# Weight splitting, copy placement and instruction order in an attention and two-MoE kernel

## The chip, the cores and the metric

The kernel runs on one core of one Trainium2 chip. The metric is the device time of one execution in microseconds, as a median over executions. Engines are called by their names and, in profile rows, by short ones: TensorE (PE, its weight loads PEld), VectorE (DVE), ScalarE (ACT), GpSimd (POOL), SyncE (SP, its queue SPq). L455 is line 455 of the kernel before.

## The reference

Three stages in float32 follow each other. Attention has 4 batches, 8 heads, 576 positions and 64 features. Its output is a coarse part (queries, keys and values averaged over groups of 4 positions, softmax attention on 144 of them, each result repeated 4 times) plus a local part (softmax over the at most 7 positions with a distance under 4). The result, 2304 tokens by 512, goes through two dense layers:

```python
h = x @ w_in                       # first MoE: 512 -> 2048
r = np.maximum(h, 0.0)
x = (s * (r * r) + b) @ w_out      # 2048 -> 512
out = ((x @ w_a) * (x @ w_b)) @ w_out2   # second MoE: 512 -> 1536 -> 512
```

The inputs of the change are the weights w_in and w_out of the first MoE. The host hands all weights over as 64-bit words (float64 bit patterns in the kernel's eyes: two 32-bit words, or four 16-bit halves).

## The kernel before, in words

TensorE multiplies in fp32r, a float32 format that it reads in rounded form. To keep float32 accuracy every operand is split into a high part (the value copied into fp32r) and a low part (the value minus its high part), and a product takes three matmuls: high by high, high by low, low by high.

The first MoE goes over six blocks of 384 tokens (BLOCKS). In each block 16 steps (a_iter) run over the 2048 hidden columns, 128 at a time: 12 matmuls make h (L1162 to L1164), ScalarE takes relu (L1179), square (L1183) and the high copy gh (L1186), VectorE the low part gl (L1190), and 12 matmuls add to four output banks (L1205 to L1207). One step needs two weight slices, one of w_in and one of w_out, so 32 slices in all; they stay in SBUF after the first block. The second MoE begins at about 504 us of the span.

A slice is prepared by w_words and w_slice, in this order: SyncE loads 512 KB (L335, w); ScalarE scales the upper words to z (L414); ScalarE moves the low bits out of the second half of each pair of words (L421); VectorE tests the sign and writes it as a half word (L426); VectorE shifts z by 3 and ors low bits and sign in (L434); ScalarE copies z to the high part (L450); VectorE subtracts for the low part (L455). RAMP_BUFS gives z two buffers.

Ahead of the first block and beside it runs attention. Batch 0 and the first 768 tokens ("ramp") are done with matmuls: down() handles the coarse part of one batch and head pair (scores L688, row maximum L702, exponential L715, transposes L739, copies L751, output L760, copy to upT L772), tile_job() the local part of 128 tokens (scores L843 and L851, maximum L878, subtraction L887, exponential L895, sum L919, division L925 and L929, transposes L937, copies L947, output L956, sum with the coarse part x L973). split_x() then makes the high part xsh on ScalarE (L569) and the low part xsl on VectorE (L573). The first three tiles feed block 0. The values of batch 1 are averaged over 4 positions by transfers: pool_in() has SyncE load two halves plainly (L621) and GpSimd add six more on top with adding transfers (L623), each one behind the one before on the same half; down(1, ...) needs them in L760. GpSimd also averages K and Q of batch 1 (L656, L657). Later tokens get their local part from VectorE alone (unit()).

The order of instructions on each engine is not written by hand. Every piece of work is a Task with an engine, an estimated duration, what it reads and writes, buffers and PSUM banks that it takes and gives back, and a due time. Program.order() simulates the engines and picks, again and again, the task that can start first; between equals the earlier due time decides. Class Wire estimates transfers and class Clock TensorE's clock. What this simulation decides is then the fixed order on every engine and every buffer's owner; engines wait on semaphores for what isn't there yet, in order. T0, LEAD and the DUE_ constants shift due times. While no h matmul has run, the simulation puts filler matmuls (L330, bf16 zeros, up to 20 at a time) in front of TensorE tasks that would otherwise leave it idle; they write a bank of the group "acc" that is held until the first h.

These lines of order() hold the rule:

```python
key = (s + t.wait, t.due - t.lead, t.num, s)
if best is None or key < best[0]:
    best = (key, t, picks, fs)
```

## Time and profile before

| what | value |
|---|---|
| runs | 928.06, 933.91, 927.93 us; median 928.06 |
| profiled execution | 933.64 us |
| its span | 931.8 us, so 1.84 us lie around the span |
| granted TensorE clock, mean over the span | 0.988 |
| TensorE busy | 909.6 us, 98% |
| VectorE busy | 781.5 us, 84% |
| ScalarE busy | 480.9 us, 52% |
| GpSimd busy | 72.4 us, 8% |
| DMA | 97.07 MB, mean 104 GB/s |

The span is the time from the first to the last instruction of the profiled execution; all stretches below count from its start. A PEclk of 1.00 is TensorE's upper level of 2.4 GHz, 0.50 its lower level of 1.2 GHz; a value between them is a mean over a stretch. Durations of neighbouring instructions on one engine overlap by a little, so what one instruction costs its engine is read from the distance between starts. A row with x2 merges two instructions of one kind.

### The profile page before, as it was taken

What the parts mean: (1) busy time and instruction counts of PE and PEld (TensorE: products, weight loads), DVE (VectorE), ACT (ScalarE), POOL (GpSimd) and SP (SyncE); (2) the same over time, 40 slices, a digit from 0 to 9 for tenths busy, and PEclk for the clock granted to TensorE, in tenths of its full rate; (3) what the DMA queues carried; (4) which work ended last, traced back from release to release, by engine and by line L of the source; (5) the groups of instructions that cost most, each with busy time, mean ns of one, the idle gap of its engine ahead of it and who ended that gap; (6) DMA issues with size and microseconds to landing.
All of it is one profiled execution on the core that took longest, in us unless ns stands there. A gap on an engine that the chain in (4) does not pass through costs nothing.

```text
span 931.8 us, 14461 instructions
## 1 busy us (share of the span) xinstructions
PE 909.6 (98%) x5456; PEld 847.6 (91%) x5456; DVE 781.5 (84%) x1383; ACT 480.9 (52%) x1017; POOL 72.4 (8%) x73
## 2 busy tenths in 40 slices
PE   8996999999999999999999999999999999999998
PEld 5685999999999899999999899998999999999997
DVE  7995898999999999995977999779877779877753
ACT  4694994335544454445987545336433336433322
POOL 0531122002222210000000000000000000000000
PEclk9997999999999999999999999999999999999999
DMA  9972936224345432314667232002200000200001
GB/s 244 273 258 62 289 89 206 82 69 128 105 118 116 133 89 69 102 29 161 213 228 256 93 107 75 23 23 102 86 23 26 26 11 35 102 23 24 1 1 68
DMA packets 47145, 97.07 MB, mean 104 GB/s; under 512 B 6396, under 2 KB 21884, under 8 KB 46692
## 3 DMA queue, kind: packets, MB, share of 16 engines
q1 hardware_dynamic: 39444, 93.09, 30.9%
q0 software_dynamic: 7200, 2.67, 2.4%
q8 instruction: 43, 0.70, 0.3%
q10 hardware_dynamic: 432, 0.39, 0.1%
q14 instruction: 26, 0.21, 0.1%
HBM read 83.54 MB, written 12.58 MB: 103 GB/s over the span
## 4 chain that ended last, share of the span: by engine, by line
PE 81%; DVE 8%; issue 5%; DMA 3%; POOL 2%; ACT 1%; SPq 0%; DVEq 0%; POOLq 0%; ACTq 0%
PE ab L1451 29%; PE acc L1205 6%; PE acc L1206 6%; PE acc L1207 6%; PE h L1162 6%; PE h L1163 5%; PE acc L1592 5%; PE h L1164 5%; PE acc L1593 5%; PE acc L1591 5%; DVE pr L1072 1%; PE o L760 1%; DMA x<-x2d 1%; DVE gl L1190 1%; DMA w<-in_qT_dram 1%
## 5 line engine op out<-in xcount | busy, mean ns | idle before, releaser
L1451 PE MATMUL ab<-xo,w 128*128 128x384 f32 x1332 | 270.2, 339 | 0.0
L1451 PEld LDWEIGHTS ab<-xo,w 128*128 128x128 f32 x1332 | 239.0, 188 | 16.0 <-DVE u L1525 1.7
L1205 PE MATMUL acc<-gh,w 128*128 128x384 f32 (+1 forms) x384 | 132.6, 345 | 1.0 <-ACT w L421 0.6
L1162 PE MATMUL h<-xsh,w 128*128 128x384 f32 x384 | 132.4, 345 | 0.0
L1206 PE MATMUL acc<-gl,w 128*128 128x384 f32 x384 | 130.1, 339 | 0.4 <-DVE gl L1190 0.4
L1207 PE MATMUL acc<-gh,w 128*128 128x384 f32 (+1 forms) x384 | 129.9, 338 | 0.0
L1163 PE MATMUL h<-xsl,w 128*128 128x384 f32 x384 | 129.8, 338 | 0.0
L1164 PE MATMUL h<-xsh,w 128*128 128x384 f32 x384 | 129.7, 338 | 0.0
L1179 ACT ACTIVATE u<-h 128x384 f32<-128x384 f32 x96 | 47.1, 491 | 124.3 <-PE h L1164 121.5
L1567 ACT ACTIVATE gh<-u 128x384 fp32r<-128x384 f32 x68 | 35.6, 524 | 86.7 <-DVE u L1528 50.2
L1205 PEld LDWEIGHTS acc<-gh,w 128*128 128x128 f32 x384 | 72.3, 188 | 4.5 <-issue 1.9
L1162 PEld LDWEIGHTS h<-xsh,w 128*128 128x128 f32 x384 | 72.6, 189 | 2.0 <-issue 1.8
L1206 PEld LDWEIGHTS acc<-gl,w 128*128 128x128 f32 x384 | 72.5, 189 | 0.9 <-DVE gl L1190 0.8
L1163 PEld LDWEIGHTS h<-xsl,w 128*128 128x128 f32 x384 | 72.8, 189 | 0.0
L1164 PEld LDWEIGHTS h<-xsh,w 128*128 128x128 f32 x384 | 72.6, 189 | 0.0
L1207 PEld LDWEIGHTS acc<-gh,w 128*128 128x128 f32 x384 | 72.5, 189 | 0.0
L1475 ACT ACTIVATE w<-ab 128x384 f32<-128x384 f32 x33 | 16.2, 491 | 100.6 <-PE ab L1451 100.5
L1190 DVE TENSOR_TENSOR gl<-u,gh 128x384 fp32r<-128x384 f32 x96 | 53.0, 552 | 11.5 <-ACT gh L1186 11.1
L1593 PE MATMUL acc<-wx,gl 128*128 128x512 f32 x141 | 55.6, 394 | 0.0
L1592 PE MATMUL acc<-wx,gh 128*128 128x512 f32 x141 | 55.4, 393 | 0.0
L1591 PE MATMUL acc<-wx,gh 128*128 128x512 f32 x141 | 55.4, 393 | 0.0
L426 DVE TENSOR_SCALAR w<-w 128x512 uint16<-128x512 f32 x59 | 42.5, 769 | 11.4 <-ACT w L421 11.4
(205 smaller groups left out, 1712.3 us busy)
## 6 DMA issues: line engine op xcount, KB each, us to landing
w<-in_w_o_dram SPq DMA_DIRECT2D x25, 512.0 KB
w<-in_w_a_dram SPq DMA_DIRECT2D x24, 512.0 KB
bk<-in_ku_dram SPq DMA_DIRECT2D x22, 320.0 KB
bk<-in_vu_dram SPq DMA_DIRECT2D x22, 320.0 KB
w<-wod SPq DMA_DIRECT2D x12, 512.0 KB
w<-in_w_b_dram SPq DMA_DIRECT2D x10, 512.0 KB
x2d<-ev SPq DMA_DIRECT2D x24, 192.0 KB
x<-x2d SPq DMA_DIRECT2D x3, 1536.0 KB
```

The lines of the kernel that those rows point to most:

```text
L1162: nc.tensor.matmul(out=st["h"], lhsT=w[:, 0, k], rhs=hi[:, k], start=(k == 0), stop=False)
L1163: nc.tensor.matmul(out=st["h"], lhsT=w[:, 0, k], rhs=lo[:, k], start=False, stop=False)
L1164: nc.tensor.matmul(out=st["h"], lhsT=w[:, 1, k], rhs=hi[:, k], start=False, stop=(k == HP - 1))
L1179: A_.activation(out=st["u"], in_=st["h"], func=ACTF.Relu)
L1190: V.tensor_tensor(out=st["lo"], in0=st["u"], in1=st["hi"][:, :n].bitcast(F32), op=ALU.subtract)
L1205: nc.tensor.matmul(out=acc, lhsT=wh, rhs=st["hi"], start=(f == 0), stop=False)
L1206: nc.tensor.matmul(out=acc[:, :n], lhsT=wh, rhs=st["lo"], start=False, stop=False)
L1207: nc.tensor.matmul(out=acc, lhsT=wl, rhs=st["hi"], start=False, stop=(f == FA - 1))
L1451: nc.tensor.matmul(out=o, lhsT=w[:, k], rhs=x, start=(not more and k + n == 0), stop=(k == 1 and n == 2), skip_group_check=more,)
L1591: nc.tensor.matmul(out=acc, lhsT=gh, rhs=w[:, 0], start=first, stop=False)
L1592: nc.tensor.matmul(out=acc, lhsT=gh, rhs=w[:, 1], start=False, stop=False)
L1593: nc.tensor.matmul(out=acc, lhsT=gl, rhs=w[:, 0], start=False, stop=last)
```

## The change

For the 32 slices of the first MoE the sign is no longer a test that writes half words. VectorE takes a bitwise and of z with the sign bit, into a new buffer sg of whole contiguous 32-bit words (two of them); ScalarE writes the low bits into the lower halves of these words; the shift and or reads sg. ScalarE's low bits now stand behind the sign, not ahead of it. The second MoE's slices keep the old way. The stage buffer is given back after the low bits, z has three buffers in place of two.

Every third high copy of a slice (H_ENG), all high copies of x in the ramp (XH_ENG) and every third copy to gh in block 0 (Q_ENG) move from ScalarE to VectorE, as copies with one source.

The order is planned anew. The planner's clock counts columns; a class Fetch estimates when TensorE's instructions arrive; adding transfers are taken to land 1.5 us later and to be seen 2 us later; from the ninth to the 96th load on SyncE a load waits in the program itself, too, until the load eight before it has landed (send). Filler matmuls may stand ahead of any TensorE task of the ramp, after the first h too, and write into the task's own bank. All due constants have new values.

```diff
+H_ENG, XH_ENG, Q_ENG = "AAD", "D", "AAD"
-POOL_PREP = 2.0
-CONST_ENG, DUE_CONST = "G", 13.6
+POOL_PREP, VISIT = 2.0, 0.2
+CONST_ENG, DUE_CONST = "G", 9.8
...
-T0, STEP = 32.0, 4.018 / 384
-LEAD = 15.2
-DUE_DOWN = (7.3, 7.1, 8.6, 17.2)
-DUE_NEXT = (57.9, 0.8)
-DUE_TILE = (5.8, 19.7, 21.3)
-DUE_JOB = (12.0, 11.2, 13.0)
-
-WARM, FILL_MIN, FILL_MAX = 18, 0, 20
-
-RAMP_BUFS = {"dq": 2, "dk": 2, "qd": 4, "kd": 4, "tq": 1, "tk": 1, "tv": 1, "e": 1, "x": 1, "z": 2}
+T0, STEP = 29.7, 4.018 / 384
+LEAD = 15.4
+DUE_DOWN = (5.3, 4.2, 19.9, 15.5)
+DUE_NEXT = (62.2, 0.6)
+DUE_TILE = (6.9, 2, 7.1)
+DUE_JOB = (9.7, 11.6, 11.0)
+
+WARM, FILLS, FILL, FILL_COLUMNS, KEEP_COLUMNS = 18, 20, 0.172, 408, 2376.3
+
+RAMP_BUFS = {"dq": 2, "dk": 2, "qd": 4, "kd": 4, "tq": 1, "tk": 1, "tv": 1, "e": 1, "x": 1, "z": 3, "sg": 2}
...
+POOL_LATE = 1.5
+RAMP_QUEUE, RAMP_LOADS, SP_WAIT = 8, 96, 0.15
...
 class Clock:
 
 
-    TICK, COLUMNS = 3.41333, 1.4
+    TICK, FIRST, COLUMNS, KEEP, FULL = 3.41333, 3360.0, 2600.0, KEEP_COLUMNS, 2400.0
+
...
+    def window(self, end):
+        total = 0.0
+        for a, b, cols in reversed(self.past):
+            if b <= end - self.TICK:
+                break
+            total += cols * (b - max(a, end - self.TICK)) / (b - a)
+        return total
...
-            work -= d * rate
-            t += d
+        self.count, self.ready, self.sent = 0, {}, []
+
+    def drain(self, t):
+        return max([b for a, b in self.sent[-24:] if a <= t], default=0.0) - DMA_LAND
+
+    def took(self, drain):
+        return self.FIRST + self.SHARE * max(0.0, drain) + self.TOOK
+
+    def run(self, clock, t, work, cols, words):
+        done = 0
+        for x in range(self.count + 1, self.count + words + 1):
+            i, j = (x + self.EARLY) // self.PART, (x + self.LATE) // self.PART - 1
+            trig, wall = i > 0 and (x + self.EARLY) % self.PART == 0, j > 0 and (x + self.LATE) % self.PART == 0
+            if not trig and not wall:
+                continue
+            n = x - self.count - done
+            t = clock.run(t, work * n / words, cols * n / words)
+            done += n
+            if trig:
+                self.ready[i] = t + self.took(self.drain(t) - t)
+            else:
+                t = max(t, self.ready.get(j, 0.0))
+        self.count += words
+        if done < words:
+            n = words - done
+            t = clock.run(t, work * n / words, cols * n / words)
         return t
 
 
...
                     if e == "POOL" and t.dma:
                         s = max(s, adding)
-                    if e == "SP" and len(landed) >= QUEUE:
-                        s = max(s, landed[-QUEUE])
+                    if e == "SP" and t.dma:
+                        q = RAMP_QUEUE if len(landed) < RAMP_LOADS else QUEUE
+                        if len(landed) >= q:
...
             if t.eng == "PE":
-                g0 = at["PE"]
-                if "acc" in t.rel:
-                    warming = False
-                while warming and t.fill < FILL_MAX and (t.fill < FILL_MIN or clock.run(g0, 0.17, 1.0, False) < s):
-                    g0 = clock.run(g0, 0.17, 1.0)
+                g0 = max(at["PE"], fs[0]) if fs else at["PE"]
+                while t.fill < t.fills:
+                    end = clock.run(g0, FILL, FILL_COLUMNS, False)
+                    if end > s and clock.window(max(s, g0) + t.dur) + t.cols >= clock.KEEP:
+                        break
+                    g0 = fetch.run(clock, g0, FILL, FILL_COLUMNS, 2)
                     t.fill += 1
...
+def copies(n):
+    return n / 1920 + 0.075
 
...
+    todo = [0]
+    loads = []
+    behind = mybir.DependencyInfo(mybir.DependencyClass.Sync, mybir.DependencyReason.DATA)
+
+    def send(out, in_):
+        made = nc.sync.dma_start(out=out, in_=in_)
+        ins = getattr(made, "ins", made)
+        if RAMP_QUEUE <= len(loads) < RAMP_LOADS:
+            tc.add_manual_dep(ins, loads[-RAMP_QUEUE].name, behind, reason="few transfers at once")
+        loads.append(ins)
+
     def bank(tag, shape, name):
-        return ps.tile(shape, F32, tag=tag, name=name, bufs=4 if tag == "acc" else 2)
-
-    pw = []
-
-    def keep_warm(count):
-
-        for _ in range(count):
...
         const_eng.tensor_copy(out=bmaskb, in_=bm_of["bm"])
 
...
 
         tz = add("ACT", 0.56, z_fn, [("st", k)], [("z", k)], acq, after=first, wait=PATIENCE)
 
+        def low_fn(out):
+            A_.activation(out=out, in_=halves()[:, :, 1], func=ACTF.Copy, scale=2.0 ** -13, bias=-4095.5 * 2.0 ** -13)
+
         def a_fn(picks):
             low = st["low"] = words()[:, :, 0]
-
-            A_.activation(out=low, in_=halves()[:, :, 1], func=ACTF.Copy, scale=2.0 ** -13, bias=-4095.5 * 2.0 ** -13)
-
-        add("ACT", 0.56, a_fn, [("st", k)], [("low", k)], wait=PATIENCE)
+            low_fn(low)
 
         def s_fn(picks):
             V.tensor_scalar(
                 out=halves()[:, :, 1], in0=words()[:, :, 1].bitcast(F32), scalar1=0.0, scalar2=32768.0, op0=ALU.is_lt, op1=ALU.mult
             )
 
-        add("DVE", 0.53, s_fn, [("low", k)], [("sg", k)], wait=PATIENCE)
+        def sw_fn(picks):
+            st["low"] = sg(picks)
+            V.tensor_scalar(
+                out=st["low"], in0=st["z"].bitcast(I32), scalar1=-(1 << 31), scalar2=None, op0=ALU.bitwise_and
+            )
+
+        def aw_fn(picks):
+            low_fn(st["low"].bitcast(U16).rearrange("p (m c) -> p m c", c=2)[:, :, 0])
+
+        done = [ld_pick(ld), "stg"]
+        if sg:
+            add("DVE", copies(DM), sw_fn, [("z", k)], [("sg", k)], [("rsg",)], wait=PATIENCE)
+            add("ACT", 0.56, aw_fn, [("st", k), ("sg", k)], [("low", k)], rel=done, wait=PATIENCE)
+        else:
+            add("ACT", 0.56, a_fn, [("st", k)], [("low", k)], wait=PATIENCE)
+            add("DVE", 0.53, s_fn, [("low", k)], [("sg", k)], wait=PATIENCE)
 
         def b_fn(picks):
             zi, low = st["z"].bitcast(I32), st["low"]
             V.scalar_tensor_tensor(out=zi, in0=zi, scalar=3, in1=low, op0=ALU.logical_shift_left, op1=ALU.bitwise_or)
 
-        add("DVE", 0.6, b_fn, [("z", k), ("sg", k)], [name], rel=[ld_pick(ld), "stg"], wait=PATIENCE)
+        add("DVE", 0.6, b_fn, [("z", k), ("low", k), ("sg", k)], [name], rel=["rsg"] if sg else done, wait=PATIENCE)
         return tz
 
     def w_slice(k, ph, lo_eng, after=()):
@@ -443,13 +548,21 @@
             st["z"] = new(ph, "z", [128, DM])
             return st["z"]
 
-        w_words(k, ("w",), z, (), ("t", k), [(ph + "z",)], after)
+        def sg(picks):
+            return new(ph, "sg", [128, DM], I32)
+
+        w_words(k, ("w",), z, (), ("t", k), [(ph + "z",)], after, sg)
+        eng = H_ENG[k % len(H_ENG)]
 
         def h_fn(picks):
             wt[k] = slot(picks[0], F32R)
-            A_.activation(out=wt[k][:, 0], in_=st["z"], func=ACTF.Copy)
-
-        add("ACT", 0.52, h_fn, [("t", k)], [("wh", k)], [("w",)], wait=PATIENCE)
+            if eng == "D":
+                V.tensor_copy(out=wt[k][:, 0], in_=st["z"])
+            else:
+                A_.activation(out=wt[k][:, 0], in_=st["z"], func=ACTF.Copy)
+
+        name, cost = ("DVE", copies(DM)) if eng == "D" else ("ACT", 0.52)
+        add(name, cost, h_fn, [("t", k)], [("wh", k)], [("w",)], wait=PATIENCE)
 
         def l_fn(picks):
...
+        eng = XH_ENG if ph == "r" else "A"
         while done < n:
             i = max(j for j, s in enumerate(starts) if s <= t0 + done)
             o = t0 + done - starts[i]
             w = min(n - done, BLOCKS[i] - o)
 
             def hi(picks, i=i, o=o, w=w, done=done):
-                A_.activation(out=xs["a", i][0][:, :, o:o + w], in_=st["x"][:, :, done:done + w], func=ACTF.Copy)
+                if eng == "D":
+                    V.tensor_copy(out=xs["a", i][0][:, :, o:o + w], in_=st["x"][:, :, done:done + w])
+                else:
+                    A_.activation(out=xs["a", i][0][:, :, o:o + w], in_=st["x"][:, :, done:done + w], func=ACTF.Copy)
 
...
-                        nc.sync.dma_start(out=pooled[b][:, kh], in_=src[:, kh, :, r])
+                        send(out=pooled[b][:, kh], in_=src[:, kh, :, r])
                     else:
                         G.dma_start(out=pooled[b][:, kh], in_=src[:, kh, :, r], accum_op=ALU.add)
 
                 t[kh] = add(
                     "POOL" if r else "SP", 1.25 if r else ISSUE, fn, (), [("pv", b)] if r == 3 else (), () if r + kh else [("pv",)], (), due,
-                    [t[kh]] if r else [t[0]] if kh else after, order=kh if r == 0 else 0, seen=0.1, dma=[wires(HK, HP, 512, 0, r > 0)],
+                    [t[kh]] if r else [t[0]] if kh else after, order=kh if r == 0 else 0, seen=2.0 if r == 3 else 0.1, dma=[wires(HK, HP, 512, 0, r > 0)],
                 )
...
 
         ts = add(
-            "PE", 0.7, s_fn, [("qd", key), ("kd", key)], [("sc", key)], [wide, wide, E_SLOT[ph]],
-            [ph + "qd", ph + "kd"], lead=LEAD, share=0.5)
+            "PE", 0.7 + (VISIT if b > 1 else 0), s_fn, [("qd", key), ("kd", key)], [("sc", key)], [wide, wide, E_SLOT[ph]],
+            [ph + "qd", ph + "kd"], lead=LEAD, cols=648, fills=FILLS if ph == "r" else 0, words=16)
...
             st["hi"] = pools[""].tile([128, NU], F32R, tag="gh", name="gh", bufs=n_bufs[""]["g"])[:, :n + ext]
             A_.activation(out=st["u"], in_=st["u"], func=ACTF.Square)
 
...
-            A_.activation(out=st["hi"][:, :n], in_=st["u"], func=ACTF.Copy)
+            if eng == "D":
+                V.tensor_copy(out=st["hi"][:, :n], in_=st["u"])
+            else:
+                A_.activation(out=st["hi"][:, :n], in_=st["u"], func=ACTF.Copy)
 
         def l_fn(p):
             st["lo"] = pools[""].tile([128, NU], F32R, tag="gl", name="gl", bufs=n_bufs[""]["g"])[:, :n]
@@ -1192,7 +1315,9 @@
                 V.tensor_copy(out=st["hi"][:, n:n + 2], in_=ones)
 
         add("ACT", act(n, True), r_fn, [("h", idx)], [("u", idx)], [("u",)], ["h"])
-        chain("ACT", [(act(n), q_fn), (act(n), q2_fn)], [("u", idx)], [("gh", idx)], acq=[("g",)])
+        add("ACT", act(n), q_fn, [("u", idx)], [("uu", idx)], [("g",)])
+        name, cost = ("DVE", copies) if eng == "D" else ("ACT", act)
+        add(name, cost(n), q2_fn, [("uu", idx)], [("gh", idx)])
         add("DVE", dve(n) + (0.07 if ext else 0), l_fn, [("gh", idx)], [("gl", idx)], rel=["u"])
```

## Rows read from the trace of the kernel before

**Rows 1.** Busy time by stretch (us, busy of each engine, PEclk, DMA share, GB/s).
```profile
23.70:139.40 115.70, 103.56 (x917) 91.25 (x916) 99.31 (x211) 94.58 (x210) 32.50 (x28) 0.93 0.68 195
...
50.00:56.00 6.00, 5.29 (x67) 4.73 (x68) 4.90 (x13) 5.08 (x16) 2.60 (x3) 0.72 0.52 100
...
55.00:75.00 20.00, 19.45 (x152) 18.62 (x151) 20.00 (x45) 19.88 (x43) 2.90 (x2) 0.98 0.88 300
...
75.80:85.20 9.40, 1.45 (x9) 0.62 (x8) 2.99 (x8) 0.97 (x2) 2.48 (x2) 0.71 0.27 32
85.20:93.80 8.60, 8.60 (x47) 7.48 (x45) 4.44 (x8) 4.93 (x11) 0.11 (x1) 0.53 0.21 53
...
200.00:300.00 100.00, 99.73 (x621) 95.22 (x620) 95.02 (x130) 49.78 (x125) 22.88 (x22) 1.00 0.41 110
```
**Rows 2.** Waits of TensorE over the span (total us, times, longest).
```profile
PE o L760 <- DMA pv<-in_vd_dram: 8.0, 2, 4.3
...
PE acc L1205 <- ACT w L421: 0.6, 1, 0.6
```
**Rows 3.** TensorE in order of time (start, duration, line, idle before).
```profile
47.18 0.44 PE L1162 MATMUL h<-xsh,w 128*128 128x384 f32 x1
...
50.71 0.71 PE L688 MATMUL sc<-kd,qd 64*72 64x144 f32 x8 [2.16 <-POOL qd L657]
...
80.16 0.75 PE L760 MATMUL o<-w,pv 72*64 72x144 f32 x4 [4.32 <-DMA pv<-in_vd_dram]
84.54 0.75 PE L760 MATMUL o<-w,pv 72*64 72x144 f32 x4 [3.63 <-DMA pv<-in_vd_dram]
```
**Rows 4.** Waits of ScalarE, 47 to 150 us.
```profile
ACT up L772 <- PE o L760: 10.7, 3, 8.6
```
**Rows 5.** GpSimd in order of time: two additions, three of the six adding transfers of batch 1.
```profile
25.62 0.67 POOL L656 TENSOR_TENSOR dk<-dk 128x288 f32<-128x288 f32 x1 [3.91 <-DMA dk<-in_kT_dram]
...
32.00 1.33 POOL L623 DMA_DIRECT2D pv<-in_vd_dram  x1 [0.27 <-DMA pv<-in_vd_dram]
...
44.96 1.25 POOL L656 TENSOR_TENSOR dk<-dk 128x288 f32<-128x288 f32 x1 [2.53 <-DMA dk<-in_kT_dram]
...
50.60 1.22 POOL L623 DMA_DIRECT2D pv<-in_vd_dram  x1
...
80.34 1.20 POOL L623 DMA_DIRECT2D pv<-in_vd_dram  x1 [3.27 <-issue]
```
**Rows 6.** VectorE in order of time: before the first h, then a dense stretch.
```profile
44.30 0.68 DVE L973 TENSOR_TENSOR x<-o,up 128x512 f32<-128x512 f32 x1
...
46.66 0.68 DVE L573 TENSOR_TENSOR xsl<-x,xsh 128x512 fp32r<-128x512 f32 x1
...
62.30 1.28 DVE L434 SCALAR_TENSOR_TENSOR z<-z,w 128x512 int32<-128x512 int32 x2
63.54 1.37 DVE L426 TENSOR_SCALAR w<-w 128x512 uint16<-128x512 f32 x2
64.72 0.71 DVE L455 TENSOR_TENSOR w<-z,w 128x512 fp32r<-128x512 f32 x1
...
67.19 1.29 DVE L434 SCALAR_TENSOR_TENSOR z<-z,w 128x512 int32<-128x512 int32 x2
```
**Rows 7.** ScalarE in order of time, the same dense stretch.
```profile
62.84 1.23 ACT L421 ACTIVATE w<-w 128x512 int32<-128x512 uint16 x2
...
64.91 0.61 ACT L450 ACTIVATE w<-z 128x512 fp32r<-128x512 f32 x1
65.42 0.51 ACT L1186 ACTIVATE gh<-u 128x384 fp32r<-128x384 f32 x1
```
**Rows 8.** SyncE's queue in order of time: first and last of ten weight loads.
```profile
54.08 0.41 SPq L335 DMA_DIRECT2D w<-in_w_o_dram  x1
...
61.66 0.33 SPq L335 DMA_DIRECT2D w<-in_w_a_dram  x1
```
**Rows 9.** VectorE, one line: first and last subtraction of the 32 slices.
```profile
L455 DVE TENSOR_TENSOR w<-z,w x32: 636/688/757, 33.6 to 139.4; 128x512 fp32r<-128x512 f32 x32
```

More of the change, by code (lines that the diff above doesn't have):

```diff
@@ L94 @@
     __slots__ = (
-        "eng", "dur", "fn", "deps", "succ", "acq", "picks", "rel", "due", "lead", "share", "num", "left", "ready", "start",
-        "end", "fill", "seen", "dma", "order", "wait",
+        "eng", "dur", "fn", "deps", "succ", "acq", "picks", "rel", "due", "lead", "cols", "fills", "num", "left", "ready", "start",
+        "end", "fill", "seen", "words", "dma", "order", "wait",
     )
 class Clock:
-    TICK, COLUMNS = 3.41333, 1.4
-    def __init__(self):
-        self.done = {}
@@ L108, in run @@
-    def run(self, start, work, share, keep=True):
-        t = start
-        while work > 1e-9:
-            k = int(t / self.TICK + 1e-6)
-            rate = 1.0 if self.done.get(k - 1, 0.0) >= self.COLUMNS else 0.5
-            d = min(work / rate, (k + 1) * self.TICK - t)
-            if keep:
-                self.done[k] = self.done.get(k, 0.0) + d * rate * share
-            work -= d * rate
-            t += d
+    TICK, FIRST, COLUMNS, KEEP, FULL = 3.41333, 3360.0, 2600.0, KEEP_COLUMNS, 2400.0
@@ new lines, in __init__, with rate, run @@
+    def __init__(self, phase=0.0):
+        self.done, self.phase, self.warm, self.past = {}, phase, False, []
+    def rate(self, k):
+        if self.done.get(k - 1, 0.0) >= (self.COLUMNS if self.warm else self.FIRST):
+            return 1.0
+        return 0.5
+    def run(self, start, work, cols, keep=True):
+        t, left, warm = start, work, self.warm
+        while left > 1e-9:
+            k = int((t + self.phase) / self.TICK + 1e-6)
+            rate = self.rate(k)
+            d = min(left / rate, (k + 1) * self.TICK - self.phase - t)
+            if keep:
+                self.done[k] = self.done.get(k, 0.0) + d * rate * cols / work
+                warm = warm or rate == 1.0
+            left -= d * rate
+            t += d
+        if keep:
+            self.warm = warm
+            self.past.append((start, t, cols))
+            del self.past[:-200]
+        return t
@@ L146, in __init__, with add @@
         self.free = {k: [0.0] * n for k, n in free.items()}
-    def add(self, eng, dur, fn, reads=(), writes=(), acq=(), rel=(), due=1e9, after=(), lead=0.0, share=1.0, seen=None, dma=(), order=0, wait=0.0):
+    def add(self, eng, dur, fn, reads=(), writes=(), acq=(), rel=(), due=1e9, after=(), lead=0.0, cols=0.0, fills=0, words=12, seen=None, dma=(), order=0, wait=0.0):
         t = Task()
@@ L320, in new @@
         return pools[ph].tile(shape, dtype, tag=tag, name=tag, bufs=n_bufs[ph][tag])
-    def bank(tag, shape, name):
-        return ps.tile(shape, F32, tag=tag, name=name, bufs=4 if tag == "acc" else 2)
-    pw = []
-    def keep_warm(count):
-        for _ in range(count):
-            nc.tensor.matmul(out=pw[0], lhsT=wz[:, :128], rhs=wz, start=True, stop=True)
+    todo = [0]
[7 more added lines that the diff above has]
+        loads.append(ins)
+    def bank(tag, shape, name):
+        whole = ps.tile([128, 512], F32, tag=tag, name=name, bufs=4 if tag == "acc" else 2)
+        for _ in range(todo[0]):
+            nc.tensor.matmul(out=whole[:, :408], lhsT=wz[:, :128], rhs=wz, start=True, stop=True)
+        todo[0] = 0
+        n = 1
+        for k in shape[1:]:
+            n *= k
+        part = whole[:shape[0], :n]
+        if len(shape) == 3:
+            part = part.rearrange("p (a b) -> p a b", b=shape[2])
+        if len(shape) == 4:
+            part = part.rearrange("p (a b c) -> p a b c", b=shape[2], c=shape[3])
+        return part
     def load(dst_src, nbytes, reads=(), writes=(), acq=(), rel=(), due=1e9, after=(), rows=128, pieces=1, base=0):
@@ L860, in tile_job @@
             [("tsc", i)], [WIDE, WIDE, ("re", "w")], () if kept else ["rtq", "rtk"],
-            after=[mm["dS", bl, hp] for hp in range(HP)], lead=LEAD, share=0.55,
+            after=[mm["dS", bl, hp] for hp in range(HP)], lead=LEAD, cols=1400, fills=FILLS if ph == "r" else 0, words=32 * NQ + 4 * (1 if len(set(variant)) == 1 else NQ),
         )
@@ L1166, in a_iter @@
             prev = [mm["h", idx, 0]] if half else ([mm["h", idx - 1, 1]] if idx else [])
[L1167 removed]
+            rel = []
             if half and f == FA - 1:
```

60 lines of the change are left out of this document (37 added, 23 removed).

## The prediction

> **What bounds the kernel now.** I read the busy times by stretch first. From 200 to 300 us TensorE is busy for 99.73 of 100 us at a granted clock of 1.00 [rows 1]: in the body nothing but fewer matmuls would help, and the change takes none away. So what can be gained lies in the ramp and in block 0, up to about 139 us, where the clock falls below 1.00.
>
> Next the waits of TensorE and its order in time. Once the first h matmul has started at 47.18 us, TensorE should never stop. It stops for 2.16 us at 48.5 (Q of batch 1 isn't averaged yet), and for 4.32 and 3.63 us around 80 us, where the output of batch 1 waits for the two halves of the averaged values, pv [rows 2, 3]. After each stop it runs on its lower level. A mean clock of 0.72 over the 6 us from 50 means 2 x 0.28 x 6 = 3.4 us at 1.2 GHz, half of which, 1.7 us, is lost. A mean of 0.53 over the 8.6 us from 85.2 means 8.1 us at 1.2 GHz, 4.0 us lost; of the 1.45 us of work from 75.8 to 85.2 some 0.7 is lost [rows 1]. So pv costs 8.0 + 4.0 + 0.7 = 12.7 us, Q costs 2.2 + 1.7 = 3.9, and one wait for low bits from ScalarE costs 0.6 [rows 2]: 17.2 us behind the first h.
>
> Why is pv late? GpSimd's adding transfers go one behind the other: the first is issued at 32.00, the second only at 50.60, since four averagings for Q and K stand between them, the sixth at 80.34, and its data releases TensorE at 84.54 [rows 3, 5]. While TensorE waits, ScalarE does too: its next instruction reads that output (10.7 us, L772), and what is behind it on the engine stands, the weight slices among it [rows 4].
>
> Third, the suppliers. From 55 to 75 us VectorE is busy for 20.00 of 20 us and ScalarE for 19.88 [rows 1]. Block 0 thus has three engines near their limit, and a stop taken from TensorE pays only as far as the two others can deliver slices sooner. From 23.7 us to the last slice's subtraction at 139.4 [rows 9], 115.7 us, VectorE is busy for 99.3 and ScalarE for 94.6 [rows 1].
>
> **The change part by part.**
> *Sign.* Two signs in a row start at 63.54, what follows at 64.72: 0.59 us each [rows 6]. No row shows a bitwise and of one source over whole words. Its ends are 0.59 us (no gain) and half of it, 0.30, if two elements go at a time; above 0.59 I see no reason, as nothing is added. Two shifts with or, which read two tensors, also cost only (63.54 - 62.30) / 2 = 0.62 [rows 6]: the engine reads two streams at that pace, and a one-source operation uses only one. I take 0.34, near the low end, since some of each instruction is fixed. 32 slices x 0.25 = 8.0 us off VectorE.
>
> The Trainium skill (VectorE: DVE Perf Modes, The perf-mode tier table) says that copies and one-tensor operations on float32 in SBUF run at two elements a cycle and two-tensor ones at one; its 1227 ns for 2048 elements makes some 0.3 us for 512, an estimate. The rows at 0.62 us agree with the second half; no run here shows the first.
>
> *Copies moved.* They are 10 of 32 slices (every third), 6 tiles and 5 of the 16 gh copies. A high copy on ScalarE costs 65.42 - 64.91 = 0.51 us [rows 7], so ScalarE loses 10 x 0.51 + 6 x 0.51 + 5 x 0.39 (384 of 512 columns) = 10.1 us. VectorE gains, at the sign's two ends, 16 x 0.34 + 5 x 0.26 = 6.7 us or 16 x 0.59 + 5 x 0.44 = 11.6. I take 6.7.
>
> *Low bits and shift.* Same count and size; cost 0 as durations, between a loss and gain of 0.1 us each. The new thing is an order of three hops (sign on VectorE, low bits on ScalarE, shift on VectorE); behind a waiting low-bits instruction stand ScalarE's relu and gh, for which VectorE and TensorE wait. That is a rival below.
>
> *First h.* The third tile's sum starts at 44.30 and its low part at 46.66 [rows 6], 2.36 us, because the high copy goes round by ScalarE. On one engine it is 0.62 + 0.34: 1.4 us sooner (1.1 at the high end).
>
> *Order.* Due times for batch 1's inputs move from 32.0 + 64.3 - 57.9 = 38.4 to 29.7 + 64.3 - 62.2 = 31.8 us, and an adding transfer counts as landing later, so L760 should stand further back on TensorE. I expect both stops and their cold stretches to go: 17.2 us.
>
> *Loads.* Ten weight loads are issued within 7.6 us [rows 8], ahead of what moves (300 GB/s, [rows 1]). With the new wait, eight loads of 0.52 MB stay in flight, 4.2 MB or 14 us of transfer at that rate, which covers the wait; behind it stand all later loads of SyncE, and GpSimd's additions behind the plain pv loads. I take 0, from 1 us lost to 1 us gained (less in flight beside the adding transfers).
>
> *Fillers after the first h* stand where the plan sees a wait. If that wait doesn't come they cost: 20 of them, at the diff's figure of 0.172 us, 3.4 us. I take 0.
>
> *Sum.* TensorE alone would gain 17.2 + 1.4 = 18.6 us. VectorE is busy for 99.3 - 8.0 + 6.7 = 98.0 of 115.7 us, so its last slice can come at most 17.7 sooner; ScalarE, with 84.5 busy, is no bound. So VectorE is late next. At the 95% that it reaches from 200 to 300 us [rows 1] 98.0 takes 103.2 and the gain is 12.5; at the gapless 20 us of 55 to 75 it is 17.7. I allow 1 us of gaps, since the large waits of VectorE came with ScalarE standing at L772: 16.7 us. Against the profiled execution, 931.8 + 1.84 = 933.64, that gives **916.9 us**. The profiled execution lies 5.6 us above the median of 928.06, as one of the three runs does (933.91). I take it that this scatter comes with the pv stop and goes with it, so the sum isn't lowered again.
>
> **The rivals.**
> *The whole ramp starts earlier.* T0 is 2.3 us lower. If the first h and VectorE's slices both come 2.3 us sooner still, the gain is 18.6 + 2.3 = 20.9: 912.7 us. For: the new due times touch everything ahead of 47 us. Against: T0 only shifts due times, which break ties.
>
> *pv still ends last.* From the first addition to the release are 84.5 - 32.0 = 52.5 us. Begun 6.6 us sooner at the same pace, it ends at 77.9. TensorE, without Q's stop, the 0.6 and the 1.4, would stand there at 75.8 - 5.9 = 69.9, wait 8.0 us and run cold for 4.0 of loss: of 18.6 only 6.6 is left, 927.0 us. For: GpSimd's work suffers beside VectorE's; one addition took 0.67 us at 25.62 and 1.25 at 44.96 [rows 5]. Against: the plan now adds 1.5 + 2 us to such landings.
>
> The Trainium skill (SBUF — State Buffer, Who interferes with whom) speaks against the change here: a VectorE copy in a two-port mode takes a port pair that GpSimd needs, descriptors of its transfers included, for the whole instruction. By that rule each of the six additions could wait for one new copy, 6 x 0.34 = 2.0 us in all, an estimate, on top of 77.9. The two durations of rows 5 would agree with such a lock; no row shows it.
>
> *The bitwise and and the copies run at one element a time.* VectorE then has 99.3 + 11.6 = 110.9 us of work: gain 4.8, 928.8 us.
>
> *The sg buffers set the pace (slower).* There are two. Slices came one per (139.4 - 33.6) / 31 = 3.41 us [rows 9]; two buffers keep that pace if one is held for 6.8 us. Low bits at 62.84 were shifted in at 67.19 [rows 6, 7]; with the sign ahead of it and the shift's own time that makes about 6.0. The forecast needs (105.8 - 16.7) / 31 x 2 = 5.7. Above 6.8 the kernel is slower; held for 7.3 us, each slice takes 0.25 us more, 31 x 0.25 = 7.8: 941.4 us. For: ScalarE is full from 55 to 75. Against: it has 10.1 us less to do, and the planner knows the buffers.
>
> **How the numbers follow.** The forecast (VectorE's limit, 914 to 921 us) gets 0.48, the earlier ramp 0.22, pv 0.12, the slow mode 0.06, sg 0.12. A difference of about 1% is what a measurement of this kernel can tell from none; faster by more is below 918.8. Some 0.31 of the forecast's 0.48 lies below, with the earlier ramp 0.53. Slower than 937.3 is most of sg: 0.10. The rest, 0.37, is within 1%. The range from 907 to 930 us leaves out sg and the tail of the earlier ramp. Blocks 1 to 5 and the second MoE get a new order too; they have 0.3 us per 100 to gain [rows 1], and I take 2 us either way.
>
> **What would show it.** In the profile after: the sign at 0.3 to 0.4 us from start to start; no wait of TensorE for pv or for Q over 1 us; a clock of 1.00 from the first h to the end of block 0; the last slice's subtraction at about 123 us in place of 139.4; VectorE over 95% busy until then, ScalarE near 85%. A wait of L760 for pv of several microseconds means the second rival, VectorE idle behind low bits that wait for a free sg the fourth. I am wrong if those stops are gone and block 0 still ends where it did.

## The result and the profile after

The kernel after took 921.01 us in the median (919.41 to 922.26, 5 runs), the one before 928.06 beside it (926.42 to 933.91, 5 runs): a ratio of 0.9907, interval 0.9885 to 0.9929 (estimated from all runs; the two medians alone give 0.9924). The interval leaves out 1, so the gain of 0.9% is real, but it is under the 1% to which I had given 0.37; I had given 0.53 to more than that. The median lies 4.1 us above the forecast of 916.9, at the very edge of its band (914 to 921 us). The profiled execution took 921.53 us, its span 918.9 us (931.8 before). The scatter went with the stops: the runs of after lie within 3 us, those of before within 8.

First the suppliers in the ramp. Busy time by stretch of the kernel after (us, busy of each engine, PEclk, DMA share, GB/s):

```profile
23.70:122.30 98.60, 94.45 (x898) 84.98 (x895) 97.04 (x231) 87.43 (x189) 27.09 (x25) 1.00 0.79 223
...
45.80:124.80 79.00, 77.34 (x608) 73.76 (x607) 75.63 (x176) 71.99 (x146) 12.96 (x10) 1.00 0.71 204
...
200.00:300.00 100.00, 99.08 (x614) 93.41 (x613) 92.00 (x139) 49.03 (x131) 23.79 (x23) 1.00 0.42 113
```

The first row ends where the last slice's subtraction starts. It answers to the first of [rows 1], 115.7 us long: 17.1 us are gone. VectorE, the third busy time, leaves 1.6 us of it unused, and the clock is 1.00 where it was 0.93. The second row goes from the first h to the first h of block 1: there TensorE too is busy for 77.34 of 79.00 us. The last row is the one to be wary of: 99.08 where [rows 1] had 99.73.

Next the operations themselves, by line (count, min/median/max in ns, first and last start in us):

```profile
L522 DVE TENSOR_SCALAR sg<-z x32: 374/419/485, 28.0 to 119.2; 128x512 int32<-128x512 int32 x32
...
L560 DVE CAST w<-z x10: 387/420/550, 47.1 to 117.6; 128x512 fp32r<-128x512 f32 x10
...
L509 ACT ACTIVATE sg<-w x32: 758/781/816, 28.4 to 119.9; 128x512 uint16<-128x512 uint16 x32
L509 ACT ACTIVATE w<-w x29: 647/670/693, 437.4 to 558.9; 128x512 int32<-128x512 uint16 x29
```

A duration takes in the tail that overlaps the next instruction, so prices are read from start to start. VectorE in order of time in a dense stretch:

```profile
64.00 0.42 DVE L522 TENSOR_SCALAR sg<-z 128x512 int32<-128x512 int32 x1
64.33 0.42 DVE L560 CAST w<-z 128x512 fp32r<-128x512 f32 x1
64.67 0.42 DVE L522 TENSOR_SCALAR sg<-z 128x512 int32<-128x512 int32 x1
65.00 0.68 DVE L568 TENSOR_TENSOR w<-z,w 128x512 fp32r<-128x512 f32 x1
65.61 1.28 DVE L539 SCALAR_TENSOR_TENSOR z<-z,sg 128x512 int32<-128x512 int32 x2
```

The sign and the copy take 0.33 and 0.34 us each, the two-source subtraction 0.61. The sign took 0.59 before [rows 6]. Counted to the start of the next instruction and added up over the 32 slices, the sign went from 18.8 to 10.9 us.

Last the waits. TensorE's longest over the whole span, then, from 45 to 125 us, what ScalarE and VectorE wait for each other over sg (total us, times, longest):

```profile
PE ab L1576 <- DVE w L1640: 1.8, 1, 1.8
PE o L1074 <- ACT w L1065: 1.2, 1, 1.2
PE acc L1330 <- ACT w L869: 1.1, 1, 1.1
```

```profile
ACT sg L509 <- DVE sg L522: 1.7, 1, 1.7
```

```profile
DVE z L539 <- ACT sg L509: 0.6, 1, 0.6
```

The 8.0 us for pv of [rows 2] have left the list, and so has the stop for Q; the three rows head it now. The 10.7 us in which ScalarE stood for that output [rows 4] are gone with them.

**Where the rest went.** Block 1's first h starts at 124.8 us (141.9 before): 17.1 us sooner. The last additions of block 5 start at 495.6 (508.7): only 13.1 sooner. Between the two, blocks 1 to 5 take 370.8 us with the same 2,194 matmuls for which the kernel before takes 366.8. So 4.0 us of the gain are given back where TensorE is the bound. Busy time of that stretch, kernel before and kernel after:

```profile
141.90:508.70 366.80, 365.61 (x2194) 356.27 (x2193) 332.33 (x493) 198.73 (x446) 38.14 (x38) 1.00 0.42 130
```

```profile
124.80:495.60 370.80, 368.04 (x2194) 355.74 (x2194) 332.45 (x493) 198.32 (x446) 40.41 (x38) 1.00 0.42 129
```

Nothing is added there (the other engines' work is the same) and the clock is 1.00 in both. What differs is the waits of TensorE's weight loads for data; the longest of them, before and after:

```profile
PEld acc L1206 <- DVE gl L1190: 0.8, 1, 0.8
```

```profile
PEld acc L1331 <- DVE gl L1313: 2.7, 8, 0.6
...
PEld bt L1220 <- ACT e L833: 0.9, 1, 0.9
PEld bt L1220 <- DVE o L1205: 0.9, 1, 0.9
PEld at L857 <- ACT u L1297: 0.8, 1, 0.8
PEld at L857 <- DVE e L848: 0.6, 1, 0.6
```

All that wait for data (not "issue") come to 3.1 us before and 7.0 after. A matmul stays "busy" while its weights are late, so the waits of TensorE itself (1.2 and 2.8 us) show less than half of the loss.

### The profile page after: what moved, and what is told of

Same layout as the page of the kernel before. It is cut to its first block, busy times and chain, and to the rows that moved or that the text cites. A ratio compares the mean times of both kernels' runs of the same rounds, so it can differ in the third digit from the quotient of the medians.

```text
span 918.9 us, 14438 instructions
## 1 busy us (share of the span) xinstructions
PE 903.5 (98%) x5437; PEld 841.1 (92%) x5437; DVE 779.5 (85%) x1404; ACT 472.9 (51%) x996; POOL 71.2 (8%) x73
## 4 chain that ended last, share of the span: by engine, by line
PE 69%; DVE 23%; issue 4%; ACT 2%; DMA 2%; SPq 0%; DVEq 0%; ACTq 0%
PE ab L1576 29%; PE acc L1717 5%; PE acc L1718 5%; PE acc L1716 5%; PE acc L1330 4%; PE acc L1331 4%; PE acc L1332 4%; PE h L1280 4%; PE h L1281 3%; PE h L1282 3%; DVE pr L1129 3%; DVE gl L1313 2%; DVE pr L1190 2%; DVE s L1135 2%; DVE pr L1197 1%
## 5 line engine op out<-in xcount | busy, mean ns | idle before, releaser
L1576 PE MATMUL ab<-xo,w 128*128 128x384 f32 x1318 | 267.5, 339 | 0.0
L1718 PE MATMUL acc<-wx,gl 128*128 128x512 f32 x156 | 61.4, 394 | 0.0
L1717 PE MATMUL acc<-wx,gh 128*128 128x512 f32 x156 | 61.3, 393 | 0.0
L1716 PE MATMUL acc<-wx,gh 128*128 128x512 f32 x156 | 61.3, 393 | 0.0
L1301 ACT ACTIVATE u<-u 128x384 f32<-128x384 f32 x96 | 50.1, 522 | 2.0
```

The lines of the kernel that those rows point to most:

```text
L1301: A_.activation(out=st["u"], in_=st["u"], func=ACTF.Square)
L1576: nc.tensor.matmul(out=o, lhsT=w[:, k], rhs=x, start=(not more and k + n == 0), stop=(k == 1 and n == 2), skip_group_check=more,)
L1716: nc.tensor.matmul(out=acc, lhsT=gh, rhs=w[:, 0], start=first, stop=False)
L1717: nc.tensor.matmul(out=acc, lhsT=gh, rhs=w[:, 1], start=False, stop=False)
L1718: nc.tensor.matmul(out=acc, lhsT=gl, rhs=w[:, 0], start=False, stop=last)
```

## Experiments: what the new operations are worth

In both, every engine's order is that of the kernel after.

**The sign reads two tensors.**

```diff
-V.tensor_scalar(out=st["low"], in0=z, scalar1=-(1 << 31), scalar2=None, op0=ALU.bitwise_and)
+V.scalar_tensor_tensor(out=st["low"], in0=z, scalar=-(1 << 31), in1=z, op0=ALU.bitwise_and, op1=ALU.bitwise_and)
```

> The changed kernel with the order of every engine untouched; only the sign's bitwise and is made to read z twice (z and mask and z), so that it should cost about 0.60 us from start to start in place of 0.33, 32 x 0.27 = 8.6 us more work for VectorE. Theory V (VectorE is at its limit in block 0, so the one-source form is what lets the new order pay): the last slice's subtraction moves from 122.3 to about 130 us, the time goes up by 7 to 9 us, to 928 to 930. Rival T (TensorE's own work is the limit and VectorE has slack): up by 0 to 2 us, to 921 to 923.

927.77 us (10 runs; ratio to before 0.9992, 0.9975 to 1.0008), 6.8 us above the kernel after and 0.2 us under theory V's range.

**The 21 copies on VectorE read two tensors.**

```diff
-V.tensor_copy(out=wt[k][:, 0], in_=st["z"])
+V.tensor_tensor(out=wt[k][:, 0], in0=st["z"], in1=st["z"], op=ALU.max)
```

(the tile and gh copies likewise)

> The changed kernel with the order untouched; the 21 copies that moved to VectorE read their source twice (maximum of a tile with itself), 0.60 us in place of 0.33 for 512 columns, 16 x 0.27 + 5 x 0.20 = 5.3 us more for VectorE. Theory V: up by 4 to 5 us, to 925 to 926. Rival T: up by 0 to 1 us.

925.05 us (4 runs; 0.9949, 0.9932 to 0.9967), 4.0 us above, as theory V has it.

The windows from 23.7 us to the last slice's subtraction, first of the doubled sign, then of the doubled copies:

```profile
23.70:131.30 107.60, 98.09 (x902) 86.59 (x901) 105.03 (x232) 89.08 (x189) 29.03 (x25) 0.98 0.73 208
```

```profile
23.70:127.70 104.00, 97.65 (x941) 85.81 (x938) 102.32 (x232) 88.28 (x191) 26.62 (x25) 1.00 0.75 214
```

VectorE has 8.0 and 5.3 us more work than the 97.04 of after, the last slice comes 9.0 and 5.4 us later, and in all three kernels VectorE idles for only 1.6 to 2.6 us of its window. What is added to VectorE's work is added to the time up to the last slice. That less work would be gained in the same way is not shown: from the first h on TensorE leaves only 1.7 us unused in the kernel after. By the Trainium skill (VectorE: DVE Perf Modes, The perf-mode tier table) copies and operations of one tensor with a constant on float32 in SBUF run at two elements a cycle; the copy's 0.34 us against 0.60 for two tensors agrees, and the bitwise and on whole integer words goes at the copy's pace (0.33 us).

**The copies stay on ScalarE**, planned anew.

```diff
-H_ENG, XH_ENG, Q_ENG = "AAD", "D", "AAD"
+H_ENG, XH_ENG, Q_ENG = "AAA", "A", "AAA"
```

> The kernel after with the 10 high copies, 6 tile copies and 5 gh copies left on ScalarE (the bitwise and stays; the order planned anew). In the kernel after VectorE is busy for 97.0 of the 98.6 us from 23.7 us to the last slice's subtraction and ScalarE for 87.4; without the copies VectorE has 16 x 0.34 + 5 x 0.27 = 6.8 us less and ScalarE 10.1 more, 97.5. Theory V (VectorE's work sets block 0's end, and what leaves it is gained until ScalarE is as full): the two change places, ScalarE is the one without gaps, the last slice within 2 us of 122.3 and the median 919 to 924. Rival S (ScalarE's longer chain, low bits and high copy, paces the slices and stops TensorE): waits of TensorE for ScalarE of over 3 us, the last slice at 126 or later and 925 to 932.

928.52 us (10 runs; 0.9999, 0.9979 to 1.0019). Two of its windows:

```profile
40.00:60.00 20.00, 16.43 (x119) 12.69 (x118) 19.31 (x44) 17.97 (x48) 7.09 (x6) 0.71 1.05 333
60.00:80.00 20.00, 19.93 (x114) 19.55 (x113) 16.62 (x34) 20.00 (x40) 3.60 (x3) 1.00 0.71 208
```

The engines do change places (ScalarE 20.00 of 20 us, VectorE 16.62), as theory V has it, and the last slice comes at 125.0, between the two theories. But the first h starts at 52.8 us instead of 45.8 and the clock is 0.71 around it, so block 1 starts at 132.7. The time is the rival's, and TensorE waits for ScalarE by 2.2 and 1.4 us as it says: with the bitwise and alone in this plan nothing is left of the gain. But from the first h to block 1 it takes 79.9 us where the kernel after takes 79.0, so 7.0 of the 7.9 us by which block 1 is later are lost ahead of the first h:

```profile
23.70:52.80 29.10, 23.43 (x313) 16.34 (x309) 29.10 (x71) 23.05 (x64) 14.56 (x15) 0.82 1.04 294
```

VectorE, from which the copies were taken, is the engine without a gap there: 29.1 us of its work stand between 23.7 us and the first h, against 22.1 in the kernel after, so the new plan puts other work there. How much of the late first h is the copies and how much that plan, this run can't say.

## Experiments: order and edits

**The new order alone** (the old sign, all copies on ScalarE, planned anew).

> The changed kernel's planner and due times, but the old sign (a test into half words, behind the low bits) and all copies on ScalarE; the planner knows these costs. ScalarE is busy for about 87 us between 23.7 and 122.3 us in the changed kernel; 10.1 more fills these 98.6 us. Theory V with ScalarE as the second supplier: no stop for pv, but slices come 4 to 6 us later than in the changed kernel, 924 to 927 us. Rival O (the new order brings it all): 920 to 922. Rival E (the edits bring it all): 927 to 929.

**The edits alone** (the planner and due times of before, the new sign, copies and buffers).

> The kernel before, its planner and due times, with the new sign, the copies on VectorE and the buffers for them (z 3, sg 2). Theory: the stop for pv stays, since nothing moves L760 or GpSimd's additions, so at most a few us are gained: 924 to 929, with a wait for pv of over 5 us. Rival E (the edits bring it all): 919 to 922 and no such wait.

The order alone is slower than the kernel before: 939.64 us (4 runs; 1.0112, 1.0088 to 1.0136), a miss of 13 us. Its longest waits of TensorE and two windows:

```profile
PE o L410 <- ACT w L1065: 4.2, 2, 3.1
PE at L857 <- DVE e L848: 2.6, 5, 1.0
PE h L1280 <- ACT w L562: 2.5, 2, 2.3
```

```profile
60.00:80.00 20.00, 12.94 (x60) 10.04 (x58) 20.00 (x40) 18.19 (x35) 4.28 (x3) 0.91 0.82 258
80.00:100.00 20.00, 20.00 (x113) 17.09 (x112) 17.30 (x37) 16.97 (x36) 1.19 (x1) 0.58 0.54 155
```

VectorE has no gap at all for 20 us, TensorE stands for 7 of them and then runs at a granted clock of 0.58. The edits alone give 926.84 us (10 runs; 0.9964, 0.9944 to 0.9985). TensorE waits for pv there, as in my rival in which pv still ends last:

```profile
PE o L793 <- DMA pv<-in_vd_dram: 6.2, 2, 4.0
```

That the time is also that rival's 927.0 is luck, since its sum was for the new order. One of the ten runs took 919.90 us, at a mean clock of 0.997 where the others have 0.991 to 0.996; that pv came in time in it is likely, but no profile shows it.

Neither half is worth the whole: the edits free VectorE, the order keeps TensorE from standing for pv meanwhile. One rival stays open: the due constants of the new planner go with the new instructions, and a set chosen for the old ones was not tried, so the 939.64 us speak of these constants and not of every new order. And blocks 1 to 5 part by planner: 365.6 us with the old one and the edits, 370.3 with the new one and no edits.

**The plan's allowances for adding transfers taken away.**

```diff
-POOL_LATE = 1.5
+POOL_LATE = 0.0
-seen=2.0 if r == 3 else 0.1
+seen=0.1
```

> The kernel after with the plan's two allowances for adding transfers taken away (1.5 us on each landing, 2 us on the last of pv). Theory A (they are what puts batch 1's output behind pv's data): TensorE waits for pv by 2 to 6 us, with a clock below 1.00 behind it, median 923 to 929. Rival B (the earlier due times do it alone, pv being ready with time to spare): no wait for pv over 1 us, 920 to 922.

932.46 us (10 runs; 1.0041, 1.0018 to 1.0064): theory A, and worse than it said. The waits for pv and the clock behind them (0.76 over 12 us, so 2.9 us lost) make 7.8 of the 10.3 us by which block 1 starts later than in the kernel after; the rest is not explained.

```profile
PE o L878 <- DMA pv<-in_vd_dram: 4.9, 2, 4.1
```

```profile
78.00:90.00 12.00, 10.92 (x65) 9.89 (x66) 7.15 (x14) 7.82 (x16) 1.19 (x1) 0.76 0.37 102
```

GpSimd's adding transfers in order of time, the sixth of this kernel, then the first and the last four of the kernel after:

```profile
74.82 1.20 POOL L741 DMA_DIRECT2D pv<-in_vd_dram  x1 [5.26 <-issue]
```

```profile
27.00 1.54 POOL L741 DMA_DIRECT2D pv<-in_vd_dram  x1 [0.82 <-DMA pv<-in_vd_dram]
...
50.85 1.19 POOL L741 DMA_DIRECT2D pv<-in_vd_dram  x1 [6.42 <-issue]
62.71 1.20 POOL L741 DMA_DIRECT2D pv<-in_vd_dram  x1 [10.67 <-issue]
72.90 1.19 POOL L741 DMA_DIRECT2D pv<-in_vd_dram  x1 [8.99 <-issue]
78.24 1.20 POOL L741 DMA_DIRECT2D pv<-in_vd_dram  x1 [4.15 <-issue]
```

And their reader on TensorE, in this kernel and in the kernel after:

```profile
74.55 0.47 PE L878 MATMUL o<-w,pv 72*64 72x144 f32 x4 [0.84 <-DMA pv<-in_vd_dram]
79.08 1.71 PE L878 MATMUL o<-w,pv 72*64 72x144 f32 x12 [4.06 <-DMA pv<-in_vd_dram]
```

```profile
83.41 1.20 PE L878 MATMUL o<-w,pv 72*64 72x144 f32 x16
```

Without the allowances the sixth is issued 3.4 us sooner than in the kernel after, and TensorE waits all the same, since the reader comes 8.9 us sooner. So what removes the stop is where the reader stands. The margin is thin: here the data came 4.3 us behind the sixth issue (74.82 to 79.08), and in the kernel after the reader starts 5.2 us behind it.

**No wait of SyncE for loads in flight.**

```diff
-if RAMP_QUEUE <= len(loads) < RAMP_LOADS:
+if False:
```

> The kernel after without the new wait of SyncE for loads in flight (the plan and every order unchanged). My prediction took 0 us for it, 1 us either way: 920 to 922. Rival 1 (the wait keeps the adding transfers of pv short, so without it pv comes late again): TensorE waits 3 us or more for pv, 925 to 929. Rival 2 (the wait delays weights): 1 to 2 us faster, 919 to 920.

921.31 us (4 runs; 0.9921, 0.9901 to 0.9941) and no wait for pv: the wait is worth nothing that can be measured, as the prediction took it.

## Experiments: what blocks 1 to 5 lose

All four plan the kernel after anew. The first three change one constant, or constants of one kind. The fourth (body_old) changes both kinds of due times and the allowance and, which its expectation doesn't name, also switches off the plan's estimate of instruction arrival (Fetch) from 124 us of planned time on.

> The plan of the kernel after, with the due times of the down products and of the three kinds of late work (DUE_DOWN, DUE_JOB) of the kernel before; the ramp's edits stay. From the first h of block 1 to the last addition of block 5 the kernel before takes 366.8 us and the one after 370.8, the version with only the new order 370.3, the one with only the edits 365.6: the loss goes with the order. Theory D (these due times make it): the stretch falls to 366 to 368 us and the median to 917 to 919, ramp unchanged (block 1 starts at 125 within 1 us). Rival P (other parts of the plan make it, such as the readiness margins of VectorE's parts or the price of a change of job): stretch 370 to 372, median 920 to 922.

> The kernel after with the planner's allowance for a change of job (VISIT 0.2) at 0. Theory D: within 1 us of the kernel after, 920 to 922, stretch of blocks 1 to 5 370 to 372. Rival V (the allowance spreads work so that data come late): stretch 367 to 368, median 917 to 919.

> The kernel after with gl's first half in each tile counted as 0.77 us later for its readers in the plan (0.9 for 0.13). In the trace of after, TensorE's weight loads of acc wait 8 times for gl, 2.7 us in all, against 0.8 us once before. Theory G (these waits and the lowered clock behind them are the loss): waits for gl under 0.5 us in all, stretch of blocks 1 to 5 367 to 369, median 917.5 to 919.5. Rival (gl's waits stand where another engine would be late anyway): waits for gl gone and others in their place, stretch 370 to 371, median 920.5 to 922.

> The kernel after with the allowance for a change of job at 0 and, beside it, the due times of the kernel before for the down products and late work (DUE_DOWN, DUE_JOB). With the allowance alone at 0 the stretch from block 1's first h to block 5's last addition fell from 370.8 to 368.6 us, and TensorE's weight loads waited 3.7 us there for data against 6.4. With the old due times alone it rose to 372.3, waits 6.2 and 2.1 more before attention's tasks. Theory W (the stretch is 363 us and what TensorE's weight loads wait for data, whichever constant brings it): stretch and waits move together; if the old due times agree with the old price of 0, waits of 3 us or less, stretch 366 to 367.5, median 917.5 to 919.5. Rival: the old due times suit only the old ramp, stretch 370 to 372, median 921 to 923.

```diff
-DUE_DOWN = (5.3, 4.2, 19.9, 15.5)
+DUE_DOWN = (5.3, 4.2, 8.6, 17.2)
-DUE_JOB = (9.7, 11.6, 11.0)
+DUE_JOB = (12.0, 11.2, 13.0)
```

(late_old and body_old)

```diff
-POOL_PREP, VISIT = 2.0, 0.2
+POOL_PREP, VISIT = 2.0, 0.0
```

(visit0 and body_old)

```diff
     def run(self, clock, t, work, cols, words):
+        if t > 124.0:
+            return clock.run(t, work, cols)
```

(body_old alone)

```diff
-add("DVE", dve(n) + (0.07 if ext else 0), l_fn, [("gh", idx)], [("gl", idx)], rel=["u"])
+add("DVE", dve(n) + (0.07 if ext else 0), l_fn, [("gh", idx)], [("gl", idx)], rel=["u"], seen=0.13 if i == 0 else 0.9)
```

(gl_margin)

The waits of TensorE's weight loads in that stretch, summed over the whole list: for data, and the "issue" ones (nothing in the profile released them) where they stand before attention's transposes (at, bt), which have almost none in the kernel before. The sums in the expectations were taken from the longer waits only.

| plan | median us | blocks 1 to 5, us | waits for data | issue at at, bt | stretch less both |
|---|---|---|---|---|---|
| before | 928.06 | 366.8 | 3.1 | 0.0 | 363.7 |
| edits alone | 926.84 | 365.6 | 1.3 | 0.3 | 364.0 |
| after | 921.01 | 370.8 | 7.0 | 0.6 | 363.2 |
| old due times (late_old) | 923.13 | 372.3 | 6.2 | 2.1 | 364.0 |
| no allowance for a change of job (visit0) | 919.92 | 368.6 | 4.1 | 1.0 | 363.5 |
| later gl (gl_margin) | 921.60 | 370.0 | 5.1 | 1.6 | 363.3 |
| all three edits (body_old) | 918.78 | 367.7 | 2.8 | 1.7 | 363.2 |
| the same kernel again (body_old_more) | 917.64 | 368.6 | 3.9 | 1.7 | 363.0 |
| after without SyncE's wait (no_hold) | 921.31 | 369.7 | 5.9 | 0.6 | 363.2 |

The last column shows what the loss is: the stretch is 363.0 to 364.0 us of matmuls and what its weight loads wait, whatever the plan. The order alone, at 370.3 us, leaves 364.8.

Each stretch is that of one profiled execution. Repeats of one order say how far to trust it: no_hold, the doubled sign and the doubled copies have the order of the kernel after and take 369.7, 370.4 and 370.9 us, and the two profiles of body_old's kernel 367.7 and 368.6. So a difference of some 1 us between two plans says nothing.

Theory D falls: the old due times alone bring nothing back (372.3 us; its rival's range ended at 372). Theory G falls too: gl's waits go from 2.7 to 0.6 us, and attention's tasks wait instead:

```profile
PEld bt L1220 <- DVE o L1205: 1.6, 1, 1.6
...
PEld at L857 <- ACT u L1297: 1.1, 1, 1.1
```

visit0 gives back 2.2 of the 4.0 us, 0.6 us short of its rival V and clear of theory D, and its whole-kernel gain (1.1 us) is within the scatter of after's runs. With the two further edits of body_old the stretch is 367.7, 0.2 us above theory W's range, and the median within its 917.5 to 919.5.

**The best of them again.**

> The kernel of body_old once more, with more runs, since its interval (0.985 to 0.994) holds the kernel after's 0.9907 and its profiled run (923.4) lay 4 us above the others: in it TensorE waited 1.6 us for pv in the ramp, whose order up to 100 us is that of the kernel after. Theory W: the shorter stretch (367.7 us against 370.8) makes it some 3 us faster than the kernel after where pv is in time, so a median of 917.5 to 919, ratio 0.986 to 0.9895. Rival: a thin margin before pv costs in about one run of four what the stretch gives, ratio 0.990 to 0.992.

917.64 us (916.89 to 921.08, 6 runs; ratio 0.9892, 0.9841 to 0.9944), as theory W has it; but of the ten runs with body_old's four, six lie below 918.3 us and three above 920.8, about as often as its rival (one in four) has the thin margin cost something; of these three only body_old's was profiled. It beats the kernel before; against the kernel after the medians differ by 2.2 and 3.4 us, but the intervals of the ratios overlap, so that it is faster than after is likely and not settled. The profile of this second set:

```profile
124.90:493.50 368.60, 366.55 (x2194) 356.18 (x2193) 332.74 (x493) 198.09 (x446) 43.37 (x38) 1.00 0.42 129
```

Of 3.5 us less span than after, 2.2 lie in blocks 1 to 5, which is what the allowance alone gave back (visit0, 368.6): in this profile the old due times and the Fetch edit add nothing to it. The other 1.4 lie behind them, in the second MoE, whose instructions wait the same 1.8 us, and are the clock. After, then this kernel:

```profile
500.00:510.00 10.00, 8.18 (x37) 7.64 (x36) 8.68 (x17) 5.89 (x11) 0.00 (x0) 0.83 0.55 197
```

```profile
500.00:510.00 10.00, 8.57 (x46) 8.00 (x47) 9.99 (x21) 5.95 (x11) 0.00 (x0) 1.00 0.34 128
```

A mean of 0.83 over 10 us is 3.4 us at the lower level, 1.7 us lost. The first profile of the same kernel (body_old) has 0.83 there too, so this is the execution and not the edit. In that profiled run (923.41 us) TensorE waited 1.6 us for pv, and in gl_margin's 1.7 us: the margin before pv is thin.

## Why the prediction was right, and where not

*VectorE's limit and the sum of the ramp: right.* I had 98.0 us of VectorE work and 1 us of gaps, so 16.7 us; measured are 97.04, 1.6 and 17.1; the 1.0 us too much work and the 0.6 too few gaps partly cancel. The sign's 8.0 us (18.8 to 10.9) and the moved copies' 6.7 (6.9) came as summed. The first h comes 1.34 us sooner (1.4), so the rival of a ramp that starts another 2.3 us earlier did not come. SyncE's wait and the fillers, taken at 0, cost next to nothing (no_hold is 0.3 us off; behind the first h a single filler, of 0.35 us, stands in the kernel after).

*Both stops gone, clock at 1.00, no stop for sg: right.* VectorE waited 0.6 us for low bits, ScalarE 1.7 us for the sign.

*Why pv's stop goes: half right.* "L760 should stand further back" is what pv_early shows. The transfers themselves gain little: the first is issued 5.0 us sooner (I had 6.6), the sixth only 2.1, since two still stand 10 to 12 us behind the one ahead of them. The earlier issue alone would not have been enough; that the reader moved by just enough is thin, as pv_early and body_old show.

*"Low bits and shift ... cost 0": too low on one side.* The low bits' write into half words lasts 0.11 us longer; counted to the start of the next instruction the 32 of them take 3.1 us more on ScalarE (18.0 to 21.1), which therefore loses 7.2 us of work (94.58 to 87.43) and not 10.1; it is 89% busy, not near 85. In block 0 that hides behind VectorE.

*"Blocks 1 to 5 ... get a new order too ... I take 2 us either way": this is the term that failed.* It measured 4.0 us of loss, the bulk of what the forecast is short of. From one profiled execution to the other the gain is 12.1 us and not 16.7: 17.1 in the ramp, less 4.0 in blocks 1 to 5, 0.2 behind them and 0.8 around the span. I had read from 99.73 of 100 us that there was nothing to gain, and put the loss at no more than the gain. A full engine's idle time bounds what a new order can gain (the edits alone gained 1.2 us there), but it does not bound what it can lose. The 4.0 us are waits of weight loads; they go with the new plan, whatever the ramp does. The allowance for a change of job makes some 2 of them, give or take the 1 us by which repeats differ. What makes the rest stays open: body_old's further edits brought back 0.9 us in one profile and nothing in the other, and which part of the plan the remaining waits come from was not found. That the allowance makes the plan believe TensorE later than it is, so that data planned just in time are late, fits these runs but is argued, not shown.

*The forecast from the profiled execution: right, with some luck.* I did not lower the sum by the 5.6 us between it and the median; the runs of after scatter far less. That the scatter comes with the pv stop fits body_old, whose profiled run with such a wait is its slowest by 4 us, but it was argued and not tested.

## To carry to other kernels

Where two suppliers are full, add up the work of the fuller one and the gaps that it keeps, and not only the stops of the engine that waits: here the stops promised 18.6 us and VectorE allowed 17.7. Take a new order of a full stretch as a possible cost that its idle time doesn't bound, look there first when a gain is short, and take a second profile of the same order before you believe a difference of 1 us. A one-source form of an operation is worth looking for on a full VectorE: it took 0.33 us where the two-source one takes 0.60.

## What I had not expected of the hardware

ScalarE writes the same 512 elements more slowly into every second half word (781 ns) than into whole words (670; 671 in the ramp of the kernel before).

GpSimd's additions stretch beside VectorE, one further than [rows 5] showed (later the kernel before has one of 2.40 us as well):

```profile
24.99 0.67 POOL L774 TENSOR_TENSOR dq<-dq 128x288 f32<-128x288 f32 x1
...
35.64 2.39 POOL L774 TENSOR_TENSOR dq<-dq 128x288 f32<-128x288 f32 x1
```

From 23.7 to 50 us VectorE is busy without a gap, so beside both of them; a full VectorE alone doesn't do it (and 0.66 us is what such an addition takes at 21.55 us, with VectorE idle). What differs is VectorE's instructions, beside the first and beside the second:

```profile
24.95 0.81 DVE L996 TENSOR_REDUCE tnb<-sc 128x4 f32<-128x280 f32 x2
```

```profile
36.11 0.72 DVE L1047 TENSOR_TENSOR w<-w,tsm 128x560 f32<-128x560 f32 x1
...
36.83 0.68 DVE L568 TENSOR_TENSOR w<-z,w 128x512 fp32r<-128x512 f32 x1
```

The first reads one tensor, the other two read two tensors from SBUF. The Trainium skill (SBUF — State Buffer, Who interferes with whom) has a VectorE instruction with two inputs in SBUF contend with a GpSimd instruction that reads SBUF; these rows agree with it, but no run here took the VectorE work away from beside that addition. None of the new copies stands beside it, so of the lock by copies in my second rival these rows show nothing.
